# Converting the gate, value and output weights in turn, with batch 0's projection summed pair by pair

## The chip, the cores and the metric

The kernel runs on one core of one Trainium2 chip. The metric is the device time of one execution in microseconds (us). The profile names the engines PE (TensorE, matmuls), PEld (its weight loads), DVE (VectorE), ACT (ScalarE), POOL (GpSimd) and SP (SyncE, here the DMA queue).

## The reference, cut to what matters

```python
def _attn_ref(x, state):                       # x (8, 8, 512, 64), state (8, 8, 32, 64)
    scores = scale * x @ state^T               # tokens read the states
    xread = softmax(scores) @ state
    scores2 = scale * state @ x^T              # states read the tokens
    sread = softmax(scores2) @ x
    return concatenate([xread, sread], axis=2)

def _moe_ref(x, w_gate, w_val, w_out, rms_g):  # x (8*544, 512), weights float64
    xn = x / rms * rms_g
    g = xn @ w_gate                            # (512, 1536)
    val = xn @ w_val                           # (512, 1536)
    return (silu(g) * val @ w_out)             # (1536, 512)
```

Eight batches of 512 tokens and 32 states pass through the attention and then a gated feed-forward block with 1536 hidden columns.

## The kernel before

The weights arrive as float64 and are turned into float32 on the chip, in 18 **pieces** of 128x1024 elements. ScalarE does three operations and VectorE four for each piece. A piece of gate or of value weights, or one of output weights, serves two of the twelve hidden blocks (a **pair**). While this goes on, the kernel computes batch 0. Batches 1 to 7 follow in a fixed loop, and the states' own rows last. The opening, up to batch 1, is laid out by hand: one string gives the order in which the next step of each stream is issued.

```python
ORDER = ("aaaaaaaaaaaeddeaaaeaaeaeaaaeaaaaaeaed..."   # 356 letters, cut
         "...kpkpkkpksssSsSsSsssssSsSSsSssSSSSSSS")

# a, A: tokens of batch 0, 1 read the states     s, S: states of batch 0, 1 read the tokens
# e: exponents of a piece (ScalarE)              d: values of a piece (VectorE)
# v: a pair's own weights v (TensorE, ScalarE)   h, t, u: hidden products, silu, gating of batch 0
# p: projection of batch 0                       w: first of batch 1      k: sums of output weights

pieces = []
for mp in range(NM // 2):                         # six pairs of hidden blocks
    for dram in (moe_w_gate, moe_w_val):
        pieces.append(dram[:, 2 * P * mp:2 * P * mp + 2 * P].rearrange("(i p) f -> p i f", p=P))
for mp in range(NM // 2):                         # all output pieces last
    pieces.append(moe_w_out[2 * P * mp:2 * P * mp + 2 * P].rearrange("(m p) f -> p m f", p=P))
```

One piece on VectorE (L210 to L221 of the kernel; four operations):

```python
VE.tensor_scalar(top, hi, 0xfffff, 0x100000, op0=ALU.bitwise_and, op1=ALU.bitwise_or)
VE.scalar_tensor_tensor(out=man, in0=top, scalar=2.0 ** 32, in1=..., op0=ALU.mult, op1=ALU.add)
VE.scalar_tensor_tensor(out=ex, in0=hi, scalar=-(1 << 31), in1=ex,          # L216: the sign
                        op0=ALU.bitwise_and, op1=ALU.bitwise_or)
VE.scalar_tensor_tensor(out=dst, in0=man, scalar=2.0 ** -52, in1=ex, op0=ALU.mult, op1=ALU.mult)
```

A pair's own weights (L453), the hidden products (L498) and the projection of batch 0 (L585):

```python
def own_weights(b, mp):
    pv = [vps.tile([P, 4 * P], F32, name="pv") for e in range(2)]
    ...                                           # 8 matmuls, then two copies to v by ScalarE

def hidden(m, n, lhs, rhs):                       # fx (2 banks), fy, fz: four banks
    gp = (fx, fy)[m % 2].tile([P, S], F32, name="f")
    vp = (fx, fz)[m % 2].tile([P, S], F32, name="f")
    ...                                           # gate product, value product; silu; gating

def project_as_ready(store):
    banks = [f.tile([P, DM], F32, name="f") for f in (fx, fy, fz, fx)]
    for m in range(NM):                           # only after all hidden products: same banks
        for r, op in enumerate(banks):
            TE.matmul(out=op, lhsT=hb[:, m, P * r:P * r + P], rhs=wo[:, m, :],
                      start=(m == 0), stop=(m == NM - 1))
            ...
    for r, op in enumerate(banks):
        ot = two.tile([P, DM], F32, name="ot", tag="g")
        SE.copy(ot, op); store(r, 0, DM, ot)
```

## Time and profile before

| | before |
|---|---|
| time, median of 3 runs | 868.32 us (867.61 to 869.21) |
| span of the profiled run | 866.1 us |
| TensorE busy | 824.3 us, 95% |
| first hidden product of batch 0 (L498) starts | 35.54 us |
| TensorE idle from there to 147.4 us | 6.8 us |
| last conversion ends | 123.4 us |
| last projection matmul of batch 0 (L585) ends | 143.0 us |

A timeline row gives the start, the duration, the engine, the line of the kernel, what is written from what, the shapes and the count. In brackets stands the idle time just before the row and what ended it. A row merges neighbouring instructions of one line. Its duration includes what happens inside the row, short gaps between two rows are not marked, and a matmul counts as busy to its end even where the next one could have started earlier; this matters below. The lines of the profile that carry the argument stand in the prediction.

### The profile page before, as it was taken

Reading aid. Unit: us, or ns where it says so; the run is one execution under the profiler, and the core shown is the slowest. Engines: PE = TensorE matmul, PEld = TensorE weight load, DVE = VectorE, ACT = ScalarE, POOL = GpSimd, SP = SyncE. Lnnn points to the kernel's source line nnn. Section 1 sums busy time; section 2 is a strip of 40 time slices with the busy share of each in tenths; the row PEclk is TensorE's granted clock in tenths of the full one; section 3 lists DMA queues with packets and bytes.
Section 4 is the critical chain, followed back from the end, with each engine's and each line's share of the span. In section 5 each row is a group of like instructions: output and inputs, shape, how many; then the busy total and the mean of one; then the engine's idle time right before and its main releaser. Section 6 shows DMA issues by size and latency. Waiting matters only on the chain.

```text
span 866.1 us, 12042 instructions
## 1 busy us (share of the span) xinstructions
PE 824.3 (95%) x4806; PEld 606.6 (70%) x4806; DVE 462.1 (53%) x714; ACT 351.4 (41%) x576; POOL 154.7 (18%) x215
## 2 busy tenths in 40 slices
PE   4698999999999999999999999999999999999998
PEld 2333445767876787777876787768776787788886
DVE  4799994586136921595147723592168513651021
ACT  6798843553146412552056213641155313520110
POOL 0000031320222112221133012311132112300000
PEclk8599999999999999999999999999999999999999
DMA  9689613620432124221333023310242023301310
GB/s 287 207 296 388 242 49 88 205 98 4 112 132 98 53 49 140 104 98 41 97 124 133 4 73 130 138 49 1 98 147 98 1 73 108 140 21 37 110 48 25
DMA packets 61593, 94.11 MB, mean 109 GB/s; under 512 B 38753, under 2 KB 46433, under 8 KB 54625
## 3 DMA queue, kind: packets, MB, share of 16 engines
q1 hardware_dynamic: 59456, 92.81, 31.7%
q8 instruction: 38, 0.62, 0.3%
q10 hardware_dynamic: 2080, 0.52, 0.3%
q14 instruction: 19, 0.15, 0.1%
HBM read 78.12 MB, written 15.20 MB: 108 GB/s over the span
## 4 chain that ended last, share of the span: by engine, by line
PE 79%; DVE 12%; ACT 5%; issue 2%; DMA 1%; SPq 0%; POOL 0%; DVEq 0%; ACTq 0%
PE f L631 31%; PE f L540 23%; PE f L498 7%; PE pv L453 5%; PE f L585 5%; PE at L266 2%; ACT sq L343 1%; DVE sq L346 1%; ACT e L378 1%; DVE eS L301 1%; PE at L336 1%; PE at L350 1%; DVE m L299 1%; PE at L325 1%; DVE g L559 1%
## 5 line engine op out<-in xcount | busy, mean ns | idle before, releaser
L540 PE MATMUL f<-aT_s,v 128*128 128x256 f32 x504 | 131.7, 394 | 0.0
L540 PEld LDWEIGHTS f<-aT_s,v 128*128 128x128 f32 x504 | 89.4, 190 | 48.6 <-issue 29.3
L631 PE MATMUL f<-wo,hb 128*128 128x256 f32 x540 | 122.7, 383 | 0.0
L631 PEld LDWEIGHTS f<-wo,hb 128*128 128x128 f32 x540 | 103.0, 193 | 15.7 <-ACT ot L651 1.9
L651 ACT COPY ot<-f 128x256 f32<-128x256 f32 x60 | 19.6, 375 | 193.2 <-PE f L631 193.2
L462 ACT COPY v<-pv 128x512 f32<-128x512 f32 x96 | 51.6, 591 | 109.5 <-PE pv L453 109.5
L631 PE MATMUL f<-wt,hs 128*128 128x256 f32 x360 | 95.2, 411 | 0.0
L480 POOL TENSOR_TENSOR vs<-v 128x256 f32<-128x256 f32 x42 | 31.0, 738 | 331.0 <-ACT v L462 331.0
L540 PE MATMUL f<-aT_t,vs 128*128 128x256 f32 x336 | 87.5, 383 | 2.3 <-DVE g L559 2.3
L631 PEld LDWEIGHTS f<-wt,hs 128*128 128x128 f32 x360 | 69.9, 203 | 16.5 <-issue 4.9
L540 PEld LDWEIGHTS f<-aT_t,vs 128*128 128x128 f32 x336 | 62.8, 190 | 14.8 <-POOL vs L483 6.5
L656 DVE TENSOR_TENSOR ot<-ot,f 128x256 f32<-128x256 f32 x45 | 17.1, 418 | 104.5 <-issue 53.2
L555 DVE TENSOR_TENSOR g<-g,f 128x512 f32<-128x512 f32 x42 | 28.7, 683 | 75.0 <-PE f L540 64.6
L453 PE MATMUL pv<-w_m,stT_g 64*32 64x512 f32 x768 | 61.3, 609 | 5.9 <-DVE w_m L221 5.9
L565 ACT ACTIVATE hb<-g 128x1024 f32<-128x1024 f32 x42 | 44.4, 1057 | 31.4 <-DVE g L559 31.4
L566 DVE SCALAR_TENSOR_TENSOR hb<-hb,g 128x1024 f32<-128x1024 f32 x42 | 51.5, 1226 | 7.2 <-ACT hb L565 7.2
L498 PE MATMUL f<-aT_s,v 128*128 128x512 f32 x96 | 45.0, 625 | 1.8 <-DVE aT_s L360 1.4
L238 POOL TENSOR_TENSOR ri<-ss,mhalf 128x4 f32<-128x4 f32 x8 | 9.4, 1170 | 206.3 <-DVE ss L354 206.3
L585 PE MATMUL f<-wo,hb 128*128 128x512 f32 x96 | 42.5, 596 | 1.5 <-DVE wo L221 1.5
L540 PE MATMUL f<-aT_t,v 128*128 128x256 f32 x168 | 43.1, 379 | 0.0
L540 PE MATMUL f<-aT_s,vs 128*128 128x256 f32 x168 | 43.1, 379 | 0.0
L498 PE MATMUL f<-xsT,w_m 128*128 128x256 f32 x192 | 41.6, 379 | 0.0
(114 smaller groups left out, 1230.6 us busy)
## 6 DMA issues: line engine op xcount, KB each, us to landing
w_m<-w_d SPq DMA_DIRECT2D x48, 1024.0 KB, 4.8
x_b<-in_x_dram SPq DMA_DIRECT2D x30, 256.0 KB, 3.9
out_dram<-ot SPq DMA_DIRECT2D x56, 128.0 KB, 1.8
raw<-in_moe_w_val_dram SPq DMA_DIRECT2D x6, 1024.0 KB, 7.7
w_d<-w_m SPq DMA_DIRECT2D x6, 1024.0 KB, 5.0
raw<-in_moe_w_out_dram SPq DMA_DIRECT2D x6, 1024.0 KB, 6.8
raw<-in_moe_w_gate_dram SPq DMA_DIRECT2D x5, 1024.0 KB, 5.2
raw<-in_moe_w_gate_dram SPq DMA_DIRECT2D x2, 512.0 KB, 4.8
```

The costliest lines, as they stand in the source:

```text
L266: TE.transpose(out=tp[:, j, :], in_=xb[:, c, P * j:P * j + P], identity=ident)
L453: TE.matmul(out=pv[e][Ns * j:Ns * j + Ns, :], lhsT=stT_g[b][D * e:D * e + D, j, :], rhs=w[D * e:D * e + D, j].rearrange("p m k f -> p (m k ...
L462: SE.copy(v[:, e].rearrange("p m k f -> p (m k f)"), pv[e])
L480: GE.tensor_tensor(out=vs[:, 0], in0=a21, in1=a22, op=ALU.add)
L498: TE.matmul(out=(vp[0] if k else gp)[:, 0:n], lhsT=lhs(i, k), rhs=r, start=(i == 0), stop=(i == len(rhs) - 1))
L540: TE.matmul(out=ps[:, i, :], lhsT=lhs[:, i, :], rhs=rhs, start=(start and i == 0), stop=True, skip_group_check=True)
L555: VE.tensor_tensor(out=g[:, :, 0, :], in0=g[:, :, 0, :], in1=ys, op=ALU.add)
L565: SE.activation(out=h, in_=gate, func=ACTF.Tanh, scale=0.5)
L566: VE.scalar_tensor_tensor(out=h, in0=h, scalar=1.0, in1=gate, op0=ALU.add, op1=ALU.mult)
L585: TE.matmul(out=op, lhsT=hb[:, m, P * r:P * r + P], rhs=wo[:, m, :], start=(m == 0), stop=(m == NM - 1))
L631: TE.matmul(out=ps[:, r, :], lhsT=lhs(k)[:, P * r:P * r + P], rhs=rhs(k), start=(start and r == 0 and k == 0), stop=(k == HM - 1), skip_gr ...
L651: SE.copy(kept[r], ps[:, r, :])
```

## The change

The intent is to fill TensorE's gaps in the opening. A pair's output weights are converted right after its gate and value weights, so that batch 0's projection can be added up pair by pair between the hidden products. For this the projection keeps four banks throughout, the hidden products move to the two banks of `vps`, and the pairs' own weights of batch 0 to the two banks of `aps`. The states of batch 0 read their tokens inside the opening and not at its end. The diff, cut to its core:

```diff
-    "aaaaaaaaaaaeddeaaaeaaeaeaaaeaaaaaeaedaaaaaedadaddadadadaaaeaaedaeadvedadvavhehde"
+    "aaaaaaaadaaadeeedaasesassdsaaaassaaaeassaaaesaaaeadaddssaaadeedaaasaddaseaaeadee"
     ... (the whole string is new)
         for dram in (moe_w_gate, moe_w_val):
             pieces.append(dram[...])
-    for mp in range(NM // 2):
         pieces.append(moe_w_out[...])
@@
-        pv = [vps.tile([P, 4 * P], F32, name="pv") for e in range(2)]
+        pv = [vps.tile([P, 4 * P], F32, name="pv") if b else
+              aps.tile([P, 4 * P], F32, name="at") for e in range(2)]
@@
-    def hidden(m, n, lhs, rhs):
-        gp = (fx, fy)[m % 2].tile([P, S], F32, name="f")
+    def hidden(m, n, lhs, rhs, banks):       # batch 0: (vps, vps); at the end: as before
@@
-    def project_as_ready(store):
-        for m in range(NM):
+    def project_as_ready(banks):
+        for f in (fx, fz, fx, fy):
+            banks.append(f.tile([P, DM], F32, name="f"))
+        for m in range(NM - 2):
             for r in range(4): ...
+        for r in range(4):
+            part(NM - 2, r); part(NM - 1, r)
+            yield
+    def projected(banks, store):             # copies and stores, three of four from a spare tile
+        ot = spare[:, r] if r < 3 else two.tile([P, DM], F32, name="ot", tag="g")
@@
-        tt = aT_t[b] = seven["late"].tile([P, 3, HS], F32, name="aT_t")
+        tt = aT_t[b] = one.tile([P, 3, HS], F32, name="aT_t")
```

More of the change, by code (lines that the diff above doesn't have):

```diff
@@ L22 @@
 ORDER = (
-    "aaaaaaaaaaaeddeaaaeaaeaeaaaeaaaaaeaedaaaaaedadaddadadadaaaeaaedaeadvedadvavhehde"
-    "dhtdedheuedtdAvAeuAvdvhdAhdedehtdedhuedtedAvAuAdevdvhdAhededhdtedhuedtevdueAvdvh"
-    "AdhededhdtedhuedtevdueAvdvhAdAhdedhtdehuededtveduAvAdvhAAehAAAAAAhAAtehuedtdAeuA"
-    "ApAAeAdepdAdAdpAAdAdpAAAeApedAedpAAeddpedeAdpAepeddepdpddpddpdwwwpppkpkpkpkkpkpk"
-    "kpkpkkpksssSsSsSsssssSsSSsSssSSSSSSS"
+    "aaaaaaaadaaadeeedaasesassdsaaaassaaaeassaaaesaaaeadaddssaaadeedaaasaddaseaaeadee"
+    "davvavdedAeadAaAdehdhdtAAduehehdAtededdepvdvpddveAheeupthdAddheAdddpueeeAddetdhv"
+    "evpvdeAddeheupAdeAtedddhdduAAhAeAedtphdppAdeAAeedueAvAdAeAvpSAdpvAdhteddhhAepAed"
+    "dAudeAtdehuAdApdAepdAApAAedAvdpdevdvehAdAdehAtduedAhhepddddAvteeSSuvpdvAhepddthS"
+    "hSkAtkwukhSSupwkwSwpSkkSpkpSkkcpwScSkSckkc"
 )
@@ L77 @@
     fz = ctx.enter_context(tc.tile_pool(name="fz", bufs=1, space=PSUM))
+    seven = {"vs": ctx.enter_context(tc.tile_pool(name="sums", bufs=2))}
     early = ExitStack()
@@ L138, in home @@
     def home(k):
-        if k >= NM:
-            m = 2 * (k - NM)
-            return wo[:, m:m + 2].rearrange("p m (i f) -> p m i f", f=P)
-        mp = k // 2
-        return (w_sb[mp] if k % 2 else new_w(mp))[:, :, :, k % 2, :]
+        mp, kind = divmod(k, 3)
+        if kind == 2:
+            return wo[:, 2 * mp:2 * mp + 2].rearrange("p m (i f) -> p m i f", f=P)
+        return (w_sb[mp] if kind else new_w(mp))[:, :, :, kind, :]
     def load_piece(k):
@@ L206, in values @@
                 else:
-                    top, ex, r = (t[:, columns(k, a)] for t in (top_, exs[k], raw[k]))
+                    top, r = (t[:, columns(k, a)] for t in (top_, raw[k]))
                     hi = r[:, :, 1]
@@ L215, in values @@
                     yield
+                    ex = exs[k][:, columns(k, a)]
                     VE.scalar_tensor_tensor(out=ex, in0=hi, scalar=-(1 << 31), in1=ex,
@@ L223, in values @@
                 if a.stop == pieces[k].shape[1]:
-                    if k < NM and k % 2:
-                        nc.sync.dma_start(out=w_d[k // 2], in_=w_sb[k // 2])
+                    if k % 3 == 1:
+                        nc.sync.dma_start(out=w_d[k // 3], in_=w_sb[k // 3])
                     raw.pop(k, None)
@@ L444 @@
     HS = S // 2
-    seven = {}
     def own_weights(b, mp):
         w = w_sb.pop(b * (NM // 2) + mp)
-        pv = [vps.tile([P, 4 * P], F32, name="pv") for e in range(2)]
+        pv = [vps.tile([P, 4 * P], F32, name="pv") if b else
+              aps.tile([P, 4 * P], F32, name="at") for e in range(2)]
         for j in range(4):
@@ L483, in more_of_v @@
         GE.tensor_tensor(out=vs[:, 2], in0=a12, in1=vs[:, 1], op=ALU.subtract)
-    def hidden(m, n, lhs, rhs):
-        gp = (fx, fy)[m % 2].tile([P, S], F32, name="f")
+    def hidden(m, n, lhs, rhs, banks):
+        gp, vp = [], []
         t = []
-        vp = []
         h = hb[:, m, :]
         def products():
-            for k in range(2):
-                if k:
-                    vp.append((fx, fz)[m % 2].tile([P, S], F32, name="f"))
+            for k, to in enumerate((gp, vp)):
+                to.append(banks[k].tile([P, S], F32, name="pv" if banks[k] is vps else "f"))
                 for i, r in enumerate(rhs):
-                    TE.matmul(out=(vp[0] if k else gp)[:, 0:n], lhsT=lhs(i, k), rhs=r,
+                    TE.matmul(out=to[0][:, 0:n], lhsT=lhs(i, k), rhs=r,
                               start=(i == 0), stop=(i == len(rhs) - 1))
@@ L503, in silu @@
             t.append(two.tile([P, S], F32, name="t", tag="g"))
-            SE.activation(out=t[0][:, 0:n], in_=gp[:, 0:n], func=ACTF.Silu)
+            SE.activation(out=t[0][:, 0:n], in_=gp[0][:, 0:n], func=ACTF.Silu)
             yield
@@ L508, in gated @@
             VE.tensor_tensor(out=h[:, 0:n], in0=t[0][:, 0:n], in1=vp[0][:, 0:n], op=ALU.mult)
-            if seven and m >= HM:
+            if "s" in seven and m >= HM:
                 k = m - HM
@@ L544, in hidden_seven @@
         g = two.tile([P, 2, 2, HS], F32, name="g", tag="g")
-        c22 = seven["vs"].tile([P, 2, HS], F32, name="c22")
+        c22 = seven["c22"].tile([P, 2, HS], F32, name="c22")
         xs = fx.tile([P, 2, HS], F32, name="f")
@@ L578, in hidden_seven, with part @@
         yield
-    def project_as_ready(store):
-        banks = [f.tile([P, DM], F32, name="f") for f in (fx, fy, fz, fx)]
-        for m in range(NM):
-            for r, op in enumerate(banks):
-                TE.matmul(out=op, lhsT=hb[:, m, P * r:P * r + P], rhs=wo[:, m, :],
-                          start=(m == 0), stop=(m == NM - 1))
+    def project_as_ready(banks):
+        for f in (fx, fz, fx, fy):
+            banks.append(f.tile([P, DM], F32, name="f"))
+        def part(m, r):
+            TE.matmul(out=banks[r], lhsT=hb[:, m, P * r:P * r + P], rhs=wo[:, m, :],
+                      start=(m == 0), stop=(m == NM - 1))
+        for m in range(NM - 2):
+            for r in range(4):
+                part(m, r)
                 if r % 2:
                     yield
-        for r, op in enumerate(banks):
-            ot = two.tile([P, DM], F32, name="ot", tag="g")
-            SE.copy(ot, op)
+        for r in range(4):
+            part(NM - 2, r)
+            part(NM - 1, r)
+            yield
+    def projected(banks, store):
+        spare = seven["s"].rearrange("p (r k) f -> p r (k f)", r=3)
+        for r in range(4):
+            ot = spare[:, r] if r < 3 else two.tile([P, DM], F32, name="ot", tag="g")
+            SE.copy(ot, banks[r])
             store(r, 0, DM, ot)
-        yield
+            yield
     def open_late():
         seven["late"] = ctx.enter_context(tc.tile_pool(name="late", bufs=1))
-        seven["vs"] = ctx.enter_context(tc.tile_pool(name="late2", bufs=2))
+        seven["c22"] = ctx.enter_context(tc.tile_pool(name="late2", bufs=2))
         seven["pool"] = ctx.enter_context(tc.tile_pool(name="halves", bufs=7))
@@ L706, in of_batch_0 @@
                 parts_0[m] = hidden(m, S, lambda e, k, m=m: v_sb[0, m // 2][0][:, e, m % 2, k, :],
-                                    [aT_s[0][:, e, :] for e in range(2)])
+                                    [aT_s[0][:, e, :] for e in range(2)], (vps, vps))
             yield from parts_0[m][part]
@@ L711, in first_of_batch_1 @@
         slot_sums(1)
+        yield
         yield from own_weights(1, 0)
-    parts_0 = {}
+        yield
+    parts_0, banks_0 = {}, []
     load_state(0)
@@ L726 @@
                "h": of_batch_0(0), "t": of_batch_0(1), "u": of_batch_0(2),
-               "p": project_as_ready(store_tokens(0)), "w": first_of_batch_1(),
-               "k": weight_sums()}
+               "p": project_as_ready(banks_0), "c": projected(banks_0, store_tokens(0)),
+               "w": first_of_batch_1(), "k": weight_sums()}
     with tc.manual_schedule(engines={mybir.EngineType.PE, mybir.EngineType.DVE,
@@ L731 @@
         for stream in ORDER:
-            if stream in "wk" and not seven:
+            if stream in "ck" and "s" not in seven:
                 early.close()
@@ L763 @@
         for part in hidden(m, NT, lambda i, k: w_sb[n][:, i, m % 2, k, :],
-                           [xsT[:, i, :] for i in range(NI)]):
+                           [xsT[:, i, :] for i in range(NI)], ((fx, fx), (fy, fz))[m % 2]):
             for _ in part:
```

## The prediction

> **What bounds the kernel now.** I read the page first, to see which engine fills the span and where.
>
> ```profile
> span 866.1 us, 12042 instructions
> PE 824.3 (95%) x4806; PEld 606.6 (70%) x4806; DVE 462.1 (53%) x714; ACT 351.4 (41%) x576; POOL 154.7 (18%) x215
> PE   4698999999999999999999999999999999999998
> DVE  4799994586136921595147723592168513651021
> ```
>
> TensorE is busy for 824 of 866 us. It falls short only in the first slices, where VectorE stands at 9: there the float64 weights are turned into float32 by VectorE and ScalarE. So only the opening can give time back, and at most 42 us in all. Next, busy time by stretch (columns: stretch, its length, busy us of each engine with its instructions, then granted clock, DMA share, GB/s):
>
> ```profile
> 0.00:25.00 25.00, 10.77 (x65) 6.04 (x65) 13.07 (x24) 14.88 (x22) 0.84 (x10) 0.83 0.90 260
> 25.00:50.00 25.00, 19.16 (x73) 8.85 (x74) 19.58 (x23) 19.68 (x24) 1.86 (x1) 0.69 0.67 225
> 50.00:75.00 25.00, 22.50 (x95) 9.40 (x100) 24.76 (x28) 23.89 (x30) 0.00 (x0) 1.00 0.97 360
> 75.00:100.00 25.00, 20.88 (x102) 9.21 (x87) 22.38 (x32) 21.76 (x27) 0.00 (x0) 1.00 0.88 326
> 100.00:125.00 25.00, 25.00 (x95) 11.03 (x94) 24.59 (x26) 14.26 (x17) 2.80 (x3) 1.00 0.18 59
> ...
> 35.54:147.40 111.86, 105.08 (x452) 47.04 (x452) 97.67 (x118) 79.53 (x100) 10.35 (x9) 0.98 0.59 214
> ```
>
> From 50 to 100 us VectorE (24.76, 22.38), ScalarE and the DMA engines (share 0.97) are all nearly full, and TensorE still is busy for 43 of 50 us. After 100 us it is full. The last row holds the stretch that the change reorders: TensorE idles there for 111.86 - 105.08 = 6.8 us only. Now its timeline, to see what stands where (start, duration, work, idle time before it and its releaser):
>
> ```profile
> 35.54 9.47 PE L498 MATMUL f<-aT_s,v 128*128 128x512 f32 x16 [1.41 <-DVE aT_s L360]
> ...
> 85.77 1.09 PE L453 MATMUL pv<-w_m,stT_g 64*32 64x512 f32 x16 [2.17 <-DVE w_m L221]
> 86.79 1.10 PE L293 MATMUL at<-ident,sS 128*128 128x128 f32 x8
> 87.72 7.03 PE L498 MATMUL f<-aT_s,v 128*128 128x512 f32 x16
> 94.59 0.60 PE L325 MATMUL at<-ident,eS 128*128 128x128 f32 x4
> 96.68 1.96 PE L585 MATMUL f<-wo,hb 128*128 128x512 f32 x4 [1.49 <-DVE wo L221]
> ...
> 123.85 19.15 PE L585 MATMUL f<-wo,hb 128*128 128x512 f32 x44
> 142.84 1.04 PE L385 MATMUL at<-ident,e 128*128 128x128 f32 x8
> ```
>
> Batch 0's hidden products (L498) end at 94.6 us. Its projection (L585) starts only at 96.7, because all twelve gate and value pieces are converted before the first output piece. By then TensorE has the backlog: the last conversion ends at 123.4, and TensorE clears the projection at 142.8, then the states' path (L385, L397, L408). The first full pair of batch 1 starts with L453 at 149.5. Before 94 us the conversions release TensorE; after it, TensorE bounds.
>
> **What the Trainium skill says.** "Perfetto Trace Analysis", section Optimization Strategy, says that where the most-contended engine changes over time, "performance may be improved by interleaving those regimes". That is this change; the stretches above show the two regimes, but also that the first leaves TensorE little room. "TensorE: Matmul & The Clock Gate", Part 1, says that the array runs at half clock until about 3.4 us of sustained activity. The trace agrees: granted clock 0.50 from 20 to 40 us, and the first group of sixteen L498 takes 9.47 us against 7.13 for the next. "VectorE: DVE Perf Modes", The perf-mode tier table, lets a float32 operation with a single tensor input run at 2x and one with two at 1x. The trace has 0.69 us and 1.22 us for 1024 columns, so a piece costs 0.69 + 3 x 1.22 = 4.3 us, and reordering pieces makes none cheaper. "PSUM — Partial Sum Buffer", The four PSUM rules, says that one matmul's output is at most one bank, 512 float32 columns; the change's four accumulating 128x512 outputs therefore hold four of eight banks throughout.
>
> **The change part by part.** Nothing heavy is added or removed: same conversions, same matmuls (96 records each for hidden products and projection), same copies. I compared the instruction order of both kernels on each engine.
>
> 1. *States of batch 0 go into the opening.* Its TensorE part (0.87 + 1.07 + 0.29, starts to starts in the timeline) is 2.2 us and moves from after 142 us to before 37 us, where TensorE is idle more than half of the time. The price is that it delays the chain to the first hidden product: two reductions and a scale (1.4 us) ahead of the softmax on VectorE, L397 at half clock (some 2 us) ahead of the second L325, and the copies between. Following that chain with the trace's durations, the squares (L343) start near 26.5 instead of 24.2. Part is won back because the wait for L453 and L245 absorbs it. The first hidden product starts at about 37.0 instead of 35.5. By then VectorE has converted three pieces, as before.
>
> 2. *Output weights third in turn, projection pair by pair.* From 37.0 on each round converts three pieces: 3 x 4.3 = 12.9 us, plus two gating products (1.2) and a share of batch 1's softmax (2 to 2.5), so 16 to 17 us of VectorE. TensorE's round is 7.0 (hidden) + 6.9 (projection) + 1.0 (L453) + 1.7 (batch 1's read) = 16.6 us. They balance. Before, a round of two pieces fed TensorE 7.0 + 1.0 and a little, hence its gaps of 0.6 to 2.2 us; now there is always a projection to fill them.
>
> 3. *The sum for TensorE.* Busy from 35.54 to 147.40 is 105.1, to 149.53 it is 107.2. Take off 2.1 for the eight L540 records of batch 1 in it and 2.4 for batch 0's states and an L256 now placed earlier: 102.7 us of work. Without a wait it ends at 37.0 + 102.7 = 139.7. The same work ended at 149.53 - 2.1 = 147.4 before. **Ceiling of the gain: 7.7 us.**
>
> 4. *VectorE's sum.* After 37.0: 15 pieces x 4.3 = 64.5, ten gatings x 0.6 = 6, batch 1's softmax and squares 10: conversions end at about 118 if nothing stops VectorE, some 12 us before TensorE needs the last output piece. So VectorE is no longer the end of the path.
>
> 5. *What eats part of it.* (a) ScalarE has 14 to 15 pieces x 3.5 us plus copies, silu, squares and five table loads of 1.28 us: about 75 of 81 us. Three in-order engines, each over 90% full, with the hidden products now in two banks instead of four: the next gate product waits for the silu of the last. I allow 1.5 us, estimated from the idle of that kind seen now (ScalarE and VectorE gaps of 0.2 to 2 us). (b) The in-order DMA queue. It already waits for TensorE before it can fetch stored weights:
>
> ```profile
> SPq L136 <- PE pv L453: 22.7, 4, 18.4
> ```
>
> In the new order the fetch that needs the fifth L453 (about 104 us by the rounds above) stands ahead of the load of the last value piece. That load lands near 110 (7.7 us median, with another MB just ahead), ScalarE stops for it with a silu behind, and TensorE's next gate product waits: 2 us.
>
> 6. *Batch 0's outputs are staged in a spare tile* instead of the two shared buffers. Before, the four copies waited little (2.7 us, on TensorE), so this only frees the first pair of batch 1: 0 to 0.3 us. The slot sums move to another pool and can start earlier; POOL is off the path.
>
> Sum: 7.7 - 1.5 - 2 = 4.2 us, all before 150 us; batches 1 to 7 and the states' own feed-forward part keep their instructions. 868.3 - 4.2 = 864.1, called **864.0 us**.
>
> **The rivals.** *It wins far more* (over 17 us, more than 2%): it would need 17 us of idle TensorE time in the opening, and only 6.8 exist after 35.5. The 17 us idle before that are bound by batch 0's softmax chain, which gets longer. Some of it returns if the extra matmuls warm the clock before 37 us: up to 2.4 us (9.47 - 7.13), giving about 861.5. *Another wait takes the place of the one removed*: the three-engine lock-step of 5(a), or loads late by 5(b). For it: the DMA share of 0.97 at 50 to 75 us, and batch 2's x (1 MB) now loaded inside this stretch. Against it: the stored weights leave once per three pieces instead of two, so the stream is less dense (about 5 MB in 16.5 us, 300 GB/s, against 360 seen). Losing all the gain needs over 7.7 us of new waits; then 868 or slightly above. *The gain is given back later*: batches 1 to 7 are TensorE-bound with little idle, and a shift survives. Yet granted clock dips (0.76 at 205 to 210 us) cost about 1.7 us per batch, seen as periods of 95.4 against 93.7 us, and may fall otherwise: plus or minus 2 us.
>
> **Range and chances.** 859.5 is the ceiling gain plus a little from a warmer clock; 867.5 leaves under 1 us. Faster by over 2% would be below 851, which no term allows: 0.01. Slower by over 2% needs a new bound of 17 us: 0.02. Within 2%: 0.97.
>
> **What would show it.** Right: projection records from about 46 us on, between the hidden products; TensorE's gaps on the conversions gone from 50 to 100 us; the last conversion at 117 to 122 while TensorE works until 141 to 145; the first hidden product at 36 to 38; the second L453 of batch 1 starting 3 to 7 us before 149.5; batches 1 to 7 shifted without change. Wrong: a start of the hidden products after 39; gaps over 4 us in TensorE from 40 to 140, with gating, silu or a load as releaser; clock below 1.00 again after 45 us; batches of a different length.

## The result, and the profile after

The changed kernel takes **858.01 us** (median of 4 runs, 857.35 to 858.28), the kernel before in the same rounds 867.97 us (867.61 to 869.21). The ratio is 0.9882, 95% interval 0.9864 to 0.9899. A ratio is the mean time of one kernel's runs over the mean of the other's runs of the same rounds, so it is not quite the ratio of the medians. The gain is 10.0 us, or 1.2%: within 2%, as forecast, but the prediction said 4.2 us, and its range ended at 859.5. The prediction was wrong.

The page of the changed kernel:

```profile
span 856.3 us, 12049 instructions
PE 825.0 (96%) x4806; PEld 607.6 (71%) x4806; DVE 458.7 (54%) x718; ACT 353.1 (41%) x578; POOL 154.1 (18%) x215
PE   5799999998999999999999999999999999999998
DVE  4899995594158713692168514692169514651121
```

The busy time of each engine is within 1% of what it was. TensorE's second to fourth digits have become 7, 9, 9. Busy time by stretch (stretch, length, busy us of PE, PEld, DVE, ACT and POOL with counts, granted clock, DMA share, GB/s):

```profile
50.00:75.00 25.00, 25.00 (x97) 11.10 (x98) 24.12 (x27) 23.04 (x28) 0.00 (x0) 1.00 0.95 323
75.00:100.00 25.00, 25.00 (x91) 10.53 (x90) 23.66 (x32) 20.41 (x25) 0.00 (x0) 1.00 0.79 285
100.00:125.00 25.00, 25.00 (x95) 10.98 (x94) 23.20 (x29) 18.65 (x25) 4.44 (x4) 1.00 0.45 161
```

TensorE is busy for 25.00 of 25 us where it had 22.50 and 20.88, while VectorE and ScalarE are about as full as they were. Now TensorE's timeline in the changed kernel:

```profile
38.15 5.20 PE L496 MATMUL pv<-aT_s,v 128*128 128x512 f32 x8 [0.46 <-DVE aT_s L360]
...
47.06 1.88 PE L585 MATMUL f<-wo,hb 128*128 128x512 f32 x4
...
81.74 1.09 PE L453 MATMUL at<-w_m,stT_g 64*32 64x512 f32 x16
...
114.65 1.09 PE L453 MATMUL at<-w_m,stT_g 64*32 64x512 f32 x16
...
138.37 0.27 PE L408 MATMUL at<-ident,sr 128*128 128x128 f32 x1
138.48 1.03 PE L538 MATMUL f<-aT_s,v 128*128 128x256 f32 x4
...
140.30 1.09 PE L453 MATMUL pv<-w_m,stT_g 64*32 64x512 f32 x16
```

The first projection matmul (L585) runs at 47 us. The second L453 of batch 1, at 149.53 us before, is at 140.30. From the first hidden product to there, the list of TensorE's waits holds one line:

```profile
PE pv L496 <- DVE aT_s L360: 0.5, 1, 0.5
```

This is the 0.46 us in front of the first hidden product itself. **After it TensorE waits for nothing until batch 1 is running.** In the kernel before, the two costliest lines of the same list were (columns: who waits for whom, us in total, times, the longest):

```profile
PE pv L453 <- DVE w_m L221: 4.4, 4, 2.2
PE f L585 <- DVE wo L221: 1.5, 1, 1.5
```

The place where batch 1 begins looked like this in the kernel before:

```profile
149.53 1.04 PE L453 MATMUL pv<-w_m,stT_g 64*32 64x512 f32 x2
150.50 0.33 PE L408 MATMUL at<-ident,sr 128*128 128x128 f32 x1
150.76 1.08 PE L453 MATMUL pv<-w_m,stT_g 64*32 64x512 f32 x14
```

L453 was interrupted by the last transpose of the states' paths (L408). From the start of L453 to the L540 behind it (151.77 us) 2.24 us went by; now it is 1.02. Nothing in these rows is marked as idle, although 1.2 us were lost. (The first two L453 start 0.45 us apart and L408 another 0.52 us later; in the changed kernel the first eight start within 0.05 us. Why the two are so slow, no run shows.)

A good marker for all kernels below is therefore the **third** L453 of batch 1, behind this place: 158.64 us before, 148.19 after, a gain of 10.45 us. The spans differ by 9.8 us, so about 0.6 us are given back behind the marker. It is all in batch 1, whose waits are longer in sum: 0.17 us at L538, 0.74 at L642 (for VectorE, hs) and 1.49 at L350, against 0.39 at L540 and 1.31 at L350 before. From batch to batch the lead then is 9.85 us (start of batch 2), 11.54 (batch 3), 9.84 (batch 4) and 9.83 at the end: a dip of the granted clock, 1.7 us each time, falls into another batch, and nothing comes of it.

### The profile page after: what moved, and what is told of

Same layout as the page of the kernel before. It is cut to its first block, busy times and chain, and to the rows that moved or that the text cites. A ratio compares the mean times of both kernels' runs of the same rounds, so it can differ in the third digit from the quotient of the medians.

```text
span 856.3 us, 12049 instructions
## 1 busy us (share of the span) xinstructions
PE 825.0 (96%) x4806; PEld 607.6 (71%) x4806; DVE 458.7 (54%) x718; ACT 353.1 (41%) x578; POOL 154.1 (18%) x215
## 4 chain that ended last, share of the span: by engine, by line
PE 85%; DVE 9%; ACT 5%; issue 1%; DMA 0%; SPq 0%; POOL 0%; ACTq 0%; DVEq 0%
PE f L642 32%; PE f L538 24%; PE pv L496 5%; PE f L585 5%; PE f L496 5%; PE pv L453 4%; PE at L266 2%; ACT sq L343 1%; DVE sq L346 1%; PE at L325 1%; DVE m L372 1%; PE at L350 1%; ACT e L378 1%; DVE eS L301 1%; PE at L453 1%
## 5 line engine op out<-in xcount | busy, mean ns | idle before, releaser
L538 PE MATMUL f<-aT_s,v 128*128 128x256 f32 x504 | 131.5, 393 | 0.2 <-ACT g L555 0.2
L538 PEld LDWEIGHTS f<-aT_s,v 128*128 128x128 f32 x504 | 89.3, 189 | 49.1 <-issue 28.8
L642 PE MATMUL f<-wo,hb 128*128 128x256 f32 x540 | 122.5, 382 | 0.0
L642 PEld LDWEIGHTS f<-wo,hb 128*128 128x128 f32 x540 | 102.6, 192 | 15.7 <-ACT ot L662 1.9
L642 PE MATMUL f<-wt,hs 128*128 128x256 f32 x360 | 95.9, 413 | 0.7 <-DVE hs L573 0.7
L538 PE MATMUL f<-aT_t,vs 128*128 128x256 f32 x336 | 87.0, 381 | 1.9 <-DVE g L557 1.9
L462 ACT COPY v<-pv 128x512 f32<-128x512 f32 x84 | 45.2, 592 | 100.1 <-PE pv L453 100.1
L642 PEld LDWEIGHTS f<-wt,hs 128*128 128x128 f32 x360 | 69.9, 203 | 17.9 <-issue 4.9
L538 PEld LDWEIGHTS f<-aT_t,vs 128*128 128x128 f32 x336 | 62.9, 190 | 13.8 <-POOL vs L483 5.5
L553 DVE TENSOR_TENSOR g<-g,f 128x512 f32<-128x512 f32 x42 | 28.6, 682 | 75.1 <-PE f L538 72.7
L453 PE MATMUL pv<-w_m,stT_g 64*32 64x512 f32 x672 | 52.9, 600 | 0.0
L496 PE MATMUL pv<-aT_s,v 128*128 128x512 f32 x96 | 45.4, 612 | 0.5 <-DVE aT_s L360 0.5
L585 PE MATMUL f<-wo,hb 128*128 128x512 f32 x96 | 45.0, 600 | 0.0
L538 PE MATMUL f<-aT_t,v 128*128 128x256 f32 x168 | 43.2, 380 | 0.0
L538 PE MATMUL f<-aT_s,vs 128*128 128x256 f32 x168 | 43.1, 379 | 0.0
L557 DVE TENSOR_TENSOR g<-g,f 128x512 f32<-128x512 f32 x42 | 28.5, 677 | 26.0 <-PE f L538 23.9
```

Of the source, the lines that this page charges most:

```text
L453: TE.matmul(out=pv[e][Ns * j:Ns * j + Ns, :], lhsT=stT_g[b][D * e:D * e + D, j, :], rhs=w[D * e:D * e + D, j].rearrange("p m k f -> p (m k ...
L462: SE.copy(v[:, e].rearrange("p m k f -> p (m k f)"), pv[e])
L496: TE.matmul(out=to[0][:, 0:n], lhsT=lhs(i, k), rhs=r, start=(i == 0), stop=(i == len(rhs) - 1))
L538: TE.matmul(out=ps[:, i, :], lhsT=lhs[:, i, :], rhs=rhs, start=(start and i == 0), stop=True, skip_group_check=True)
L553: VE.tensor_tensor(out=g[:, :, 0, :], in0=g[:, :, 0, :], in1=ys, op=ALU.add)
L557: VE.tensor_tensor(out=g[:, :, 1, :], in0=g[:, :, 1, :], in1=zs, op=ALU.add)
```

## The experiments

The theories at the start, with the letters used below:

- **S**: TensorE is saturated from the first hidden product on. The end of the opening is the start of the first hidden product plus TensorE's work. Time won or lost on another engine there changes nothing, within its room.
- **M**: moving batch 0's states brings most of the gain, by its 2.2 us and by what it kept from batch 1.
- **B**: the spare tile for batch 0's outputs brings the 1.2 us where batch 1 begins.
- **R**: the three engines run in lock-step; each microsecond more on VectorE or ScalarE counts.
- **C**: the half clock at the first hidden products costs part of the gain.

Every kernel is correct except the two that leave out an operation. "Start" is the start of the first hidden product; "marker" is the third L453 of batch 1. Ratios are to the kernel before, of the same rounds, with the 95% interval.

### Controls

The changed kernel itself, in two of the five sessions: beside `states_late`, `states_only` and `ot_shared` (chip 12), and beside `warm2` (chip 9). The sessions on chips 3 and 8 have no control; their runs are compared with the controls by the ratios to the kernel before.

> The changed kernel again, unedited, as the reference for its variants of the same call. Expected 857.3 to 858.6 us, TensorE without a wait from the first hidden product (38 us) to the second L453 of batch 1 (140 us).

> The changed kernel once more, unedited, on the chip of warm2: 857 to 858.5 us.

Measured: 857.68 us, ratio 0.9868 (0.9855 to 0.9882), and 857.40 us, ratio 0.9873 (0.9859 to 0.9888). Start to marker is 109.47 us in the first control and 110.04 in the run shown above. The start itself varies between runs of this one kernel: 37.04, 37.97 and 38.15 us. Both controls list the same single wait of TensorE, 0.5 us in front of the first hidden product. So start to marker is the steadier measure, and a single profile can't resolve half a microsecond.

### The interleaving without the states

The changed kernel, with its fourteen `s` steps put at the end again.

```diff
-    "aaaaaaaadaaadeeedaasesassdsaaaassaaaeassaaaesaaaeadaddssaaadeedaaasaddaseaaeadee..."
+    "aaaaaaaadaaadeeedaaeadaaaaaaaeaaaaeaaaeadaddaaadeedaaaaddaeaaeadee..."
-    "...wkwSwpSkkSpkpSkkcpwScSkSckkc"
+    "...wkwSwpSkkSpkpSkkcpwScSkSssscsskssssksscsss"
```

> The changed kernel with batch 0's states' path moved back behind batch 1's, as the kernel before has it. Theory S (TensorE is saturated from the first hidden product on, so time is its start plus its work): the start comes back from 38.15 to about 35.5 to 36.5 us, 2.2 us of work return at the end of the opening and up to 1.3 us of waits there, so 857 to 860 us, within 1.5 us of the control. Rival M (moving the states is a main part of the gain): the start matters little and the time rises by 3 us or more, to 861 or above.

Measured: 859.27 us, ratio 0.9889 (0.9876 to 0.9903): 9.7 us faster than the kernel before, 1.6 us slower than the control, which gained 11.3 us on the same chip. Two rows of its TensorE timeline:

```profile
36.29 4.36 PE L496 MATMUL pv<-aT_s,v 128*128 128x512 f32 x8 [0.46 <-DVE aT_s L360]
...
139.91 1.36 PE L385 MATMUL at<-ident,e 128*128 128x128 f32 x8 [1.21 <-ACT e L378]
```

The start is 1.86 us earlier than in the changed kernel, because the states no longer stand in the softmax chain's way. The marker, at 149.63, is still 1.4 us later: the states' work of 2.2 us is back behind the hidden products, with a wait of 1.21 us on ScalarE in front of it. M is refuted: the interleaving without the states brings 9.7 of the 11.3 us. The second L453 of batch 1 is one unbroken row here too (at 137.60 us), though the states are still behind it, so the 1.2 us where batch 1 begins don't hang on the move of the states.

### The states without the interleaving

The kernel before, with the changed kernel's opening up to the first hidden products (states inside), then the old order. One line that picks the exponent buffer moves behind the first two VectorE steps of a piece, as in the changed kernel, since the new order needs it.

> The kernel before with only batch 0's states' path moved into the opening (the changed kernel's order up to the first hidden product, then the old order without those steps). Theory S: the start moves from 35.5 to about 38 us, which costs 2.6, and 2.2 us of work and about 1 us of waits leave the end, so 866 to 868.5 us. Rival M: the move alone is worth 3 us or more, 865 us or less.

Measured: 866.77 us, ratio 0.9977 (0.9964 to 0.999), 2.2 us faster than the kernel before. Start 36.25, marker 157.49 (158.64 before). The waits for pieces are still there (5.3 us at L454 in four waits, 1.5 us at the first projection). The second L453 of batch 1 is unbroken here as well (148.96 us). So the move of the states is worth about 2 us on its own and about 1.6 us on top of the interleaving, each only just clear of the noise.

### The outputs in the shared buffers

```diff
-            ot = spare[:, r] if r < 3 else two.tile([P, DM], F32, name="ot", tag="g")
+            ot = two.tile([P, DM], F32, name="ot", tag="g")
```

> The changed kernel with batch 0's four output copies staged in the two shared buffers again, instead of the spare tile. Theory S: 0 to 0.5 us, so 857.5 to 859. Rival B (the 1.2 us that batch 1's first pair won beyond the prediction comes from the staging): 1 us or more, 859 to 860 us, with a wait at the first pair's copies or L453 behind the stores.

Measured: 857.59 us, ratio 0.9869 (0.9854 to 0.9884), the same as the control. Start to marker 109.92 us. B is refuted.

### A lighter conversion, in both kernels

The third VectorE operation of a piece, which sets the sign (L216), is left out: some 22 us less of VectorE over 18 pieces. The result is wrong.

```diff
-                    VE.scalar_tensor_tensor(out=ex, in0=hi, scalar=-(1 << 31), in1=ex,
-                                            op0=ALU.bitwise_and, op1=ALU.bitwise_or)
```

> The kernel before without the operation that puts the sign back (L216, 1.22 us for each of 18 pieces; wrong result on purpose: weights lose their sign). Theory S: conversions no longer release TensorE, so its 6.8 us of gaps after 35.5 us go, less what remains for ScalarE and the softmax chain: 860 to 864 us. Rival R (engines in lock-step, a piece's cost counts in both kernels alike): a gain as large as in the changed kernel.

> The changed kernel without L216 (wrong result on purpose). Theory S: TensorE has no gap to lose, so only the start can move, by up to 1.5 us: 856 to 858.5 us. Rival R: every microsecond of VectorE counts in the balanced rounds, 5 us or more: 853 or less.

Measured: the kernel before falls from 868.17 to 863.36 us (ratio 0.9947, 0.9927 to 0.9968). The changed kernel stands at 856.70 us (0.9872, 0.9856 to 0.9888). Its controls, on other chips, have 0.9868 and 0.9873, so the lighter conversion gives it nothing that can be seen. TensorE's waits for gate and value pieces in the lightened kernel before, 36 to 160 us:

```profile
PE pv L451 <- DVE w_m L219: 0.7, 1, 0.7
```

They fall from 4.4 us in four waits to 0.7 in one; a wait of 1.4 us for batch 1's exponents (eS) comes up. The broken L453 where batch 1 begins stays (2.24 us again), so VectorE's load alone does not make it. In the changed kernel there was no such wait to take away: start to marker is 109.61 us. This is S's first half: faster conversion pays before and no longer after.

### A heavier conversion in the changed kernel

The sign operation is done once more: for the output pieces alone (`vector_third`, +7.3 us of VectorE) and for all pieces (`vector_twice`, +22 us).

```diff
                     VE.scalar_tensor_tensor(out=ex, in0=hi, scalar=-(1 << 31), in1=ex,
                                             op0=ALU.bitwise_and, op1=ALU.bitwise_or)
+                    if k % 3 == 2:           # this line only in vector_third
+                        VE.scalar_tensor_tensor(out=ex, in0=hi, scalar=-(1 << 31), in1=ex,
+                                                op0=ALU.bitwise_and, op1=ALU.bitwise_or)
```

> The changed kernel with L216 done twice for the six output pieces (the operation repeats itself without changing the result): 6 x 1.2 = 7.3 us more for VectorE. Theory S: the last conversion moves from 120.5 to about 128 us and is needed at 130, so 0 to 1.5 us: 857.5 to 859.5. Rival R: 5 to 7 us, 863 to 865.

> The changed kernel with L216 done twice for all 18 pieces: 22 us more for VectorE, 18 of them after the first hidden product. Theory S: the last conversion moves to about 139 or later, 9 us beyond its need, and the first hidden product 1 to 2 us: 866 to 873 us. Rival R: 18 to 22 us, 876 to 880.

Measured: 861.91 us, ratio 0.9919 (0.9895 to 0.9943), and 879.36 us, ratio 1.0128 (1.0111 to 1.0145). Against the controls' ratios that is about 4 us for 7.3, and about 22 us for 22. TensorE's waits of `vector_third`, 38 to 165 us:

```profile
PE at L456 <- DVE w_m L224: 1.2, 2, 0.6
PE pv L499 <- DVE hb L509: 1.1, 1, 1.1
```

and of `vector_twice`:

```profile
PE at L455 <- DVE w_m L223: 5.9, 4, 2.9
PE pv L498 <- DVE hb L508: 4.7, 3, 3.1
```

The waits on pieces (w_m) and on gatings (hb) are back. Here S was wrong: it had given VectorE more room, 0 to 1.5 us and 8 to 15 us of loss. R was right about the large dose; the small one lies between the two. Start to marker grows from about 110 us to 113.8 and 128.1. A part of that is the half clock in these runs (6.16 and 6.25 us for the first eight products, 4.62 in the first control); without these eight it grows by 2.8 and 17.0 us.

### A heavier ScalarE

The first ScalarE operation of each piece is done twice, +21 us of ScalarE.

```diff
                 SE.activation(out=ex.bitcast(F32), in_=hi.bitcast(F32), func=ACTF.Abs)
+                SE.activation(out=ex.bitcast(F32), in_=hi.bitcast(F32), func=ACTF.Abs)
```

> The changed kernel with ScalarE's first step of each conversion (the absolute value, 1.15 us) done twice; the result stays right. 18 x 1.15 = 21 us more for ScalarE, some 17 of them between the first hidden product and the last conversion, where it was busy for 71 of 90 us. If the allowance of the prediction for ScalarE was wrong because ScalarE has room: 0 to 3 us, 857.5 to 860.5. If ScalarE is as tight as VectorE was found to be: 10 us or more, 868 or above.

Measured: 864.84 us, ratio 0.9973 (0.9952 to 0.9994), between the two expectations. By the ratios it is some 9 us over the controls, and 7.6 us by the medians over `first_pv` on the same chip (below): about four tenths of what was added. Busy time from 40 to 130 us, first of the changed kernel:

```profile
40.00:130.00 90.00, 90.00 (x349) 38.76 (x348) 84.44 (x101) 71.22 (x88) 5.48 (x5) 0.99 0.68 236
```

then of this one:

```profile
40.00:130.00 90.00, 85.09 (x317) 36.19 (x317) 80.11 (x93) 85.62 (x99) 2.76 (x2) 0.99 0.67 236
```

In the changed kernel TensorE is busy for 90.0, VectorE for 84.4 and ScalarE for 71.2 of 90 us. With ScalarE at 85.6, TensorE drops to 85.1. Its longest wait from 36 to 165 us:

```profile
PE at L454 <- DVE w_m L222: 1.9, 1, 1.9
```

Waits for ScalarE itself, up to 1.5 us each, stand below it in the list. So ScalarE has more room than VectorE, about in the order of their busy times, but neither has much. **The changed kernel has no wait, and almost no room**: the two are different things.

### The pieces in turn, the projection at the end

The changed kernel's order of conversion, with all `p` steps put behind the last hidden product, and `k`, `c` and the last `w` steps behind them.

> The changed kernel with the pieces in turn but the whole projection of batch 0 behind the last hidden product. The prediction's rounds: VectorE needs 16 to 17 us for three pieces and TensorE has then only 9 to 10 us to do in each, so TensorE waits some 6 us a round, the hidden products end near 120 us and 41 us of projection follow: 878 to 888 us, slower than the kernel before. Rival (the order of the pieces is what counts, not the pairwise sum): 858 to 866 us.

Measured: 885.44 us, ratio 1.0202 (1.0187 to 1.0218): slower than the kernel before by 17.5 us. TensorE's costliest wait:

```profile
PE at L453 <- DVE w_m L221: 6.8, 4, 2.9
```

With the output pieces in turn, a pair takes three conversions instead of two, so each pair's gate and value pieces come later. Without the projection to fill the time TensorE waits for them, and the projection still stands at the end. So the new order of conversion pays only with the pairwise projection. The reverse, a pairwise projection with the output pieces still converted last, was not run.

### The start: states elsewhere in the chain

`first_pv` gives the first pair's own weights the `vps` banks, which are free then, so that they need not share with the transposes. `states_gap` has this too, with the opening of the kernel before and the states' steps behind the softmax chain; `states_gap2` issues the first `v` later.

```diff
-        pv = [vps.tile([P, 4 * P], F32, name="pv") if b else
+        pv = [vps.tile([P, 4 * P], F32, name="pv") if b or mp == 0 else
```

> The changed kernel with only the first pair's own weights (L453) written to the two banks of the hidden products instead of the two that the transposes of the root mean square (L245) need. Theory S (time is the start plus TensorE's work): L245 no longer waits for ScalarE's copies of v (0.7 us of idle and an L256 ahead of it), the first hidden product starts 0.5 to 1 us earlier, 856.5 to 857.5 us. If the start is not on the path: no change, 857.7.

> The changed kernel with batch 0's states' path still in the opening but behind the softmax chain, in TensorE's gaps at 24 to 33 us, and the banks of first_pv. Theory S: the states' path stays free and the start returns from about 37.5 to 36 or 36.5 us, so 1 to 2 us are gained: 855 to 857 us. Rival: the later states' copies on ScalarE and the reductions on VectorE delay the first v, so the start stays at 37 to 38 and the time at 857.7.

> As states_gap, but the first pair's own weights (L453) come behind the transposes L245, not ahead of them. Theory S: the start is within 0.8 us of states_gap, at 36 to 37 us, 855 to 857 us; the one of the two with the earlier start has the shorter time.

Measured: 857.29 us (ratio 0.9874, 0.9859 to 0.9889), 860.13 us (0.9911, 0.9897 to 0.9926) and 858.96 us (0.9894, 0.9877 to 0.991). `first_pv` is the same as the control. The attempt to shorten the start failed: it came at 38.90 and 38.29 us, not earlier than the changed kernel's. In `states_gap` VectorE now does the states' reductions and the conversion of the first value piece after the softmax chain, and that piece is written from 32.61 us on instead of 30.18. VectorE has little free time there (4.68 of the 5 us from 30 to 35 us are busy in the changed kernel). Start to marker is 110.01 us in `first_pv` and 110.20 in `states_gap2`, close to the controls, although the starts differ by 1.2 us: S's sum about holds (`states_gap2` has one wait of 0.7 us for a piece in it, and faster first products).

### The half clock at the start

`first_pv` with idle transposes of the identity ahead of the start, 36 in `warm` and 22 in `warm2`, placed in TensorE's gaps, to keep the clock up.

```diff
+    def warm():
+        while True:
+            tp = fz.tile([P, P], F32, name="f")
+            for _ in range(4):                          # 2 in warm2
+                TE.transpose(out=tp, in_=ident, identity=ident)
+            yield
```

> first_pv with 36 idle transposes of the identity on TensorE (into a bank that the projection takes later), in its gaps between 25 and 35 us, so that the granted clock does not fall back to half. Theory C (half clock costs 2 to 3 us of the opening: L350, L453 and L245 on the chain and the first hidden products): the first hidden product starts 0.5 to 1 us earlier and its group of eight takes 3.6 instead of 4.6 to 5.2 us, 854 to 856 us. Rival: the transposes stand in the way of the chain or the clock falls anyway, 857 us or more.

> As warm, with 22 idle transposes in place of 36, so that they fit into TensorE's gaps: 8 behind L336, 6 ahead of L350, 2 behind L453 and 6 behind L245. Theory C: the clock stays at full speed into the hidden products, their first group of eight takes 3.6 us and they start no later than in the changed kernel (37 to 38 us): 855 to 857 us. Rival: the chain is again held up or the clock falls to half ahead of the hidden products all the same: 857.3 us or more.

Measured: `warm` 858.20 us, ratio 0.9889 (0.9874 to 0.9904); `warm2` 856.31 us, ratio 0.9857 (0.984 to 0.9873). From TensorE's timeline of `warm`:

```profile
32.81 0.95 PE L350 MATMUL at<-ones,sq 128*128 128x1 f32 x8
...
39.46 4.96 PE L496 MATMUL pv<-aT_s,v 128*128 128x512 f32 x8 [0.43 <-DVE aT_s L360]
```

The clock was kept (L350 takes 0.95 us where it takes 1.84 in the changed kernel; the trace's clock events have 1.00 from 28.4 to 38.6 us). But the transposes held up the chain, the start came at 39.46, and by then the clock had fallen again. Fewer transposes, better placed, from `warm2`:

```profile
37.41 3.60 PE L496 MATMUL pv<-aT_s,v 128*128 128x512 f32 x8
```

and the second control:

```profile
37.97 5.62 PE L496 MATMUL pv<-aT_s,v 128*128 128x512 f32 x8 [0.46 <-DVE aT_s L360]
```

The first eight products take 3.60 instead of 5.62 us, and start to marker is 108.44 instead of 110.46 us. Taken without these eight, start to marker is 104.84 us, to within 0.01 us, in `warm2`, in both controls, in the run shown above and in `first_pv`: that is S's sum, and all that varies in it is how long the half clock lasts. **It costs 1.0 us in the first control and 2.0 us in the second.** The clock events say when full clock returns: at 38.93 us in the first control, 41.20 in the run shown above, 41.87 in the second control, 36.87 in `warm2`. C is right for this term. That the transposes brought the early return in `warm2` is likely but not shown: in `states_gap`, without them, it came at 36.78 us, and the first eight took 3.60 us as well. `warm2` is 1.1 us faster than the control of its session and the fastest correct version measured, although the intervals still overlap.

## Why the prediction was right or wrong

The prediction's sum ended TensorE's work at 37.0 + 102.7 = 139.7 us, and with 3.5 us of new waits at 143.2, against 147.4 before: a gain of 4.2 us. In the changed kernel that work ends at 138.48 us (the first L538). Term by term:

| term | predicted | measured | effect on the gain |
|---|---|---|---|
| start of the first hidden product | 37.0 us | 38.15 us | -1.15 us |
| TensorE's work from there | 102.7 us | 100.3 us (138.48 - 38.15) | +2.4 us |
| new waits | 3.5 us | 0 | +3.5 us |
| gain up to there | 4.2 us | 8.95 us (147.4 - 138.48) | +4.75 us |
| where batch 1 begins (L453, L408) | 0 | 1.2 us (2.24 - 1.02) | +1.2 us |
| later | 0 | -0.6 us or less | -0.6 us or less |

8.95 and 1.2 are 10.15 us, against 10.45 at the marker and 10.0 us in the time; the table leaves 0.3 us at the marker unexplained.

**The step that failed is step 5, the allowance of 3.5 us for new waits.** Both of its parts were zero.

5(b), the late load, rested on a fetch of stored weights that was to need the fifth L453. The DMA queue of the changed kernel (start, duration, queue, line, what is moved):

```profile
86.55 0.37 SPq L154 DMA_DIRECT2D raw<-in_moe_w_gate_dram  x1
87.01 0.46 SPq L136 DMA_DIRECT2D w_m<-w_d  x1
91.40 0.37 SPq L154 DMA_DIRECT2D raw<-in_moe_w_val_dram  x1
```

The fetch (L136) goes out at 87.01 us. It stands after the fourth L453 (81.74 us) and long before the fifth (102.24 us), so it needed the fourth at most: the prediction had counted one too far. The load of the last value piece stands right behind it and goes out at 91.40, not near 104.

5(a), the lock-step, was read from fullness: three engines over 90% busy, so waits must come. ScalarE was less full than reckoned, 68.3 of the 81 us from 37 to 118 us and not 75; VectorE was at 76.3. No hidden product waited for a silu in the two banks. For VectorE the trace shows how close it is. Five later value pieces were ready at 48.45, 62.19, 77.99, 98.67 and 113.80 us, and the L453 that use them ran at 48.87, 62.98, 81.74, 102.24 and 114.65. Three of the five had 0.4 to 0.85 us of room. Each result came in time, three of them just. The experiments with heavier engines show that R's premise, that there is little room, was right for VectorE and partly for ScalarE, but waits of 1.5 us do not follow from it: full is not late.

**Step 3's work sum was mis-sized by 2.4 us.** It took TensorE's busy time in the kernel before as work. The trace, counted from the start of one matmul to the start of the next, settles most of it. About 0.7 us is the warmer clock at the first sixteen hidden products (9.47 us before, 5.20 + 3.60 = 8.8 us after), a chance that the prediction had put among its rivals, and luck of the run: between the two controls the same term differs by 1.0 us. 0.4 us is one group of x transposes (L266) that ran before the start in the changed kernel. And 1.1 us belong to the waits themselves: among back-to-back transposes the next L266 starts after 0.11 us, but the last one ahead of a wait is busy to its end, for 0.27 us. The nine waits between the start and 143 us in the kernel before (three of them too short to be marked) come to 1.1 us in this way, **so a removed wait gave back more than its idle time**; the changed kernel has no such place. About 0.2 us remain. These rows of the whole stretch, from the start to the marker, show how little there is to see. Before:

```profile
35.54:158.64 123.10, 116.22 (x569) 54.54 (x569) 102.56 (x127) 85.08 (x109) 13.18 (x13) 0.98 0.63 219
```

After:

```profile
38.15:148.19 110.04, 110.04 (x491) 51.11 (x491) 95.83 (x120) 81.96 (x103) 12.01 (x13) 0.99 0.70 238
```

Idle time accounts for 6.88 us (123.10 - 116.22, against 0). The other 6.2 us of the busy column (116.22 - 110.04) are the 2.4 us that the prediction had taken off for the states and an L256, the 1.2 us at L453/L408, the 0.7, 0.4 and 1.1 us above, and a rest of about 0.4 us. The column alone does not tell work from a slow clock or a hidden stall.

**Step 1 was right in kind and off in size.** The start came 2.6 us later, not 1.5 (the range of 36 to 38 was just missed). The net worth of the states' move is 1.6 to 2.2 us by the two experiments on it. The 1.2 us where batch 1 begins are a gain of their own: L408 no longer interrupts L453, with either part of the change alone. The prediction had not seen that, because the rows of L453 show no idle time.

**Right:** step 2, that the rounds balance and the gaps vanish (no wait of TensorE from the start to batch 1, from 6.8 us), and with it the first projection at 47 us (about 46). `p_end` shows the other side: with the same conversions and no projection between them, TensorE waits in those rounds. Step 4: the last conversion at 120.5 us (117 to 122). Step 6: the spare tile is worth nothing (0 to 0.3). The rival of a win over 2% was rightly refused. **Wrong** in the list of signs: TensorE until 138.5 us, not 141 to 145, and the second L453 of batch 1 earlier by 9.2 us, not 3 to 7. The ceiling of 7.7 us was no ceiling: it was the idle time that showed (6.8 us) and the states' work (2.4), less the late start (1.5), and the time that did not show as idle came on top.

**Open:** why L453 was so slow around L408, and the 0.6 us given back in batch 1: the waits in which they lie are known (L642 above all), but no experiment was made on them.

## What to carry to other kernels

A ceiling made of visible idle time is not a ceiling: busy time holds stalls, half-clock stretches and the ends of matmuls ahead of waits, so compare the length of the same rows in both kernels where a reordering touches them. Don't charge a wait because engines are full; follow the results one by one, each piece's end against its use and each buffer against the matmul that frees it, and charge only what comes late. Once nothing waits, test the room as well: here 7.3 us more on VectorE already cost about 4, so a kernel so ordered shouldn't be given more work on the two other engines.

## What the Trainium skill lacked or had wrong

- No page has what a view of the granted clock shows where the trace holds no clock event. In the second control the first event stands at 41.87 us after the start of the span; the view lists 1.00 from 35 to 40 us all the same, while eight products of that stretch took 5.62 us, against 3.60 in `warm2`. The durations are the surer sign.
- "TensorE: Matmul & The Clock Gate", Part 4, says that work in the transpose mode does not engage the full clock. Here 36 float32 transposes of the identity kept it: in `warm` the clock events have 1.00 from 28.4 to 38.6 us (L350 0.95 us instead of 1.84), in `first_pv` without them 0.50 from 26.5 to 40.1 us. As far as these transposes are in that mode, which the trace does not tell, the measurement differs from the page.
- "Perfetto Trace Analysis", section Optimization Strategy, advises to interleave regimes. It lacks how to tell a balanced order from one with room: in the changed kernel TensorE waits for nothing, yet +7.3 us on VectorE cost about 4 us, +22 us about 22, and +21 us on ScalarE 8 to 9.
- No page gives the size of what TensorE's busy time hides: sixteen matmuls of L453 with one L408 among them took 2.24 us with no idle time marked, and 1.02 us without it; a transpose counts as busy for 0.27 us ahead of a wait where the next one otherwise starts after 0.11.
